# Pair 0 on two load queues with its q in two parts, and inverted sums of pairs 0 to 5 spread by TensorE

## The chip, the cores and the metric

The kernel runs on one core of one Trainium2 chip. The metric is the device time of one execution in microseconds. Three runs of the kernel before took 1489.81, 1485.3 and 1478.97 us; their median is 1485.3 us. One more execution was profiled.

## The reference

Attention with normalized q and k, for 8 batches, 12 heads, 448 tokens and 64 columns per head, and then a bilinear feed-forward block on all 3584 tokens. Everything is fp32.

```python
q_n, k_n = rmsnorm(q, g_q), rmsnorm(k, g_k)          # x / sqrt(mean(x*x) + 1e-6) * g
scores = np.matmul(q_n, k_n.transpose(0, 1, 3, 2)) / np.sqrt(64)
attn = np.exp(scores - scores.max(-1, keepdims=True))
attn = attn / (attn.sum(-1, keepdims=True) + 1e-9)
x = np.matmul(attn, v).transpose(0, 2, 1, 3).reshape(3584, 768)
out = ((x @ w_a) * (x @ w_b)) @ w_out                # 768 -> 1536 -> 768
```

The weights come as fp64 and are rounded to fp32 in the kernel.

## The kernel before

**A pair.** The attention work is cut into 24 units, which the code calls p and this text calls a pair: two pairs of heads of one batch, so four heads. Three units are one batch. For each, `loads` brings q, k and v (two DMAs each, one for each half of the partitions), `normalize` makes the inverse roots of the mean squares, `transposes` turns q and k so that the 64 head columns lie on partitions, `scores` makes seven blocks of scores and their exponentials, `values` multiplies them with v and collects in PSUM.

**Normalization.** ScalarE squares all of q (L434), VectorE reduces it to 14 sums per partition (L436) and scales them (L440), GpSimd raises them to the power -0.5 (L442), VectorE multiplies q with the result (L446). For k the same is done except for the last step: its factor goes into the scale of the exponential (L499). TensorE transposes k and the normalized q, seven blocks of 128 columns each (L472), and ScalarE copies both out of PSUM (L477, L479); the copy of q carries the gains.

**Sums over keys.** Up to pair 4 (`WIDE = 5`) TensorE sums the exponentials over the keys by a product with ones (L551) beside the value products; from pair 5 on, VectorE and GpSimd add the exponentials up first (L529), and one product with ones follows. Each of the 64 partitions of a head then holds the same sums. ScalarE copies them to the tile `rec` (L564). `invert` takes one row for each of two heads, spreads it over 56 partitions of the tile `few` by DMA (L571), VectorE inverts that (L584), a DMA stores it in DRAM (L576), and two DMAs read it back, the same row for 64 partitions each (L580), into `rec`. `divide` multiplies the outputs with it on VectorE (L622). All these DMAs are issued by the queue of SP, in order, among the loads of later pairs.

**PSUM.** The tag `sc` has two buffers of two banks; scores, transposes, and the sums of pairs from 5 on take turns in it. `o` has one (the values), `mm` two of one bank each.

**Weights.** 18 blocks of weights are loaded by ScalarE's queue (L357, L360), rounded (ScalarE L247, VectorE L248 to L256), turned into seven factors (L370) and kept in DRAM (L378, L381). They begin after set points of the attention. The feed-forward block multiplies by quarters with seven products in place of eight (`pq`, L1178; `po`, L879), in the second half of the run twice over (`da` and `dg`, L755; L1076).

**Order.** Every operation is first listed with its engine, a cost, reads and writes; the cost sets nothing any more in this file. `Plan.run` takes a list of places from the packed text `ORDER` (L32) and issues the operations in that order, so each engine's queue is written out by hand, as it were. Waits between engines follow from reads and writes.

**The start.** Five batches of warming matmuls (L1269, four matmuls each of 128 columns, two records to a matmul) run before the first data are there. The first activation (L210) makes ScalarE load its table.

Of the kernel before, what the change touches and what calls it, by code (L numbers as in the profile page):

```python
# [12 lines left out]
FP32 = mybir.dt.float32  # L13
# [7 lines left out]
def _float_of(bits):  # L21
# [11 lines left out]
    "c-rk(33OFulCJ;1>wE9+_r4`BJ4tY13kWE-Vk_=Mzy(Feg+K^|5JDoDg@lB#h!ROcSYk+k7ZAt-gzS(7hD~J+C`N^LVRUq`J$;<<X!jXCGj&5)"  # L33
    ">~_xBo;kMDP5t-X_pkMTRe$|eb)lIZ48gG44VDT<wPl!wVSubDCMZK>O_pV;RFX6)OnL?Ue!mNx-~&&A+nqmLoCL#$X2WBd6NZ@cATDlf_=D%t"
    "xd&3tOb_D{$;`y*kT^Z@O=e006CWR6z%0z0oX2!5-jlniZBcCtG%o}K>tCy^%&H_=J1VNnL92jQVGGP7WJA>&cK!PGq^x2!Dfx~RLvhi!MWenc"
    "O8pvEezjsn4HOlAQTSzHN;DsUva${9%Rbs*8iXx>AKoj2>a}#s7AWo}MX>c4uvHrZP*@2YD*x1x0sFZ2uCM>Y=)}ou;P<=X0+hBC)E6}DBzx+~"
    "&fk5svw3?vsWW%)Y5>?-4?A}3tUdtSYWHnFWYyG?YWV)Uwl3(@zTHGS=x+E5>c52Mop7OX2Q=<)gu1;u;e*=k$3CoWsVx^98p|7C+dgh9w|5Kd"
    "hiXu^(vD^-H8;|R_Qr<Yoshfdv&vRdv7@Q!gAaE?!*-}YSl<J$o~hYhhnrPH6SOuSZ)$7|Y1Uc~G&VHsYiR6hhK^NGzpJ!$N0r!8)pVq)mNx8y"
    "+W)Hk?)#m!wcEE>eNb2R$8)t2HD}LOzx&?%RquV?^X_{+pPYU7d{0l$hsp=<I0EmS2?RE8>7ko9W9{V0(|`O^ccA;5lYx^bjvwy{1kUvQ;q7;h"
    "25QfIdivD)^QTXra=mrx^r=&)1A$ZBuN{63-ad3H(0#D`WMI>q#{yp+ITm>1jV}*X9lmg3@1f5R>^;8!=+V7_qi>!+a&F&Q@#q^>@4oRypr@ni"  # L40
    "O#A6W?d^x#PwYE>@aRA9Yv0@66*%14x#z%Vou7PqY~SAVRb3yof7lT?wCBK~J?9SY-_INj1opSKoZQ=TJkZ?S@$DYy{JL{vTl@aTjV%pb7h0M-"
    "!dg1o&u?t`80uT$+=lf44SOqgy<68&54AgBdtGbwf0j3IZLF?7ux?v9l)qYMwYUGiyzD~Rzrp8g0aim}IoY(U{_LvKRb=(bnrgCADkjB6uN*r`"
    "zFD;bie7&Opl~@Xf7vqO#TNmV(!~@2K3E8OkhcI9<U(!^<PyWk1jv9F=E2+-<^q(aLwXvd&4D?o0JBpd1xzCez`hG)8UdI(1t5MhOnwfYdlsI<"
    ")lUID36tQ7Cm)B2@YqCn6drv99(fpG!gv@DMjXI{500e|*ju~qxf@{2U2xZ(aOZE~PBI#9za4Ia(d0MeR{54ux5$Ky96?45$8ClUg`u&QNnjuh"
    "0JssZ2e__3Kuk15M?q9Sh$5yDhJ;+hNHFokISBFrcs<~8gWCd&fDW3bYm`!@fG(64()|2I`H)9mS^%&hCl_+g6!6(*cDFb`hhzgVD17>o^!!D6"
    "dFcxvH!UZPKx!^zW@KkB%E*Q+an`K&b6_(`%Sz8A88BnroU#|vX3u3|R_f|mv!~DNoUS~d*qS(lBqpSigp`>ub<Wf&*@;u8O><0}o8X)}E&aKv"
    "t`siinRv(3NhQUO8PmC^xCCL+i%%})mOO#<bi>n=o_Hc*(i43A<B!jKoPT8E#BmcJdIsYD>9L7%kHtO4O?YtpqvIw&JZ{|h@sErf|9}`5_wfA_"
    "njW1n_Wp5WvGKszxUu&+#QV5=@4j1jXiVJLxG`hLaQEMJAAdjl;Jx?UkIy~ay?5MwM;kYq=YZwe+gO%&Iry7z8a51sSZ0WD_h5FAK<~JN9nG;E"
    "d+V+2D2_$_F%*UpfgmyVgDS_K2z;Xhw5xcqJidSe%Mg{Jmx{+rsoU+tit(}CR<+(in<eELgXb=lAb$|cvXo^!7R#`VVcKtwVQ`*<aq~Q)0fy}@"
    "p+UHZ2ch^(FD0f$iK<az7sdw2QQd|f#<3v?CMd{8;i1&SPy-DHp_1NWV+NLJy)dI0+K-_=g8bZscqlO}<08vGri3FpB^Ouv2?YE6cFpnvxY0lj"  # L50
    "-EPS;`3_tzXD@Hg)=jo#U#mF)b7w=^#~&xpNls1$v<pauq_^Lm38!a3clTS6cxndx;lzw-N8rsV@UIE+@dx9l?1z6rd|e;D|7<7pU~TtX?4Gvn"
    "?zXnwyW1wULdWZbG&QwBV_W0i#+D}dw5j3yCfL>1@@P}j+4@F!WGC4{-iFgV#@E!;9v@$Qblj06uod7iY~Orfb4|_W>aMPu>d))YLsye+Ra>fR"
    "2yEVZZ&lT%4L$E{J5#;w6m0C?5;y@HV8i;2W7e;$*if-<%)yF^u8Q)GP30E?yLShwssga_)z?TFR0L`(DxhNBn#%I>b?Bzx#PP~w>)))reeJr#"
    "Wrr$Y&B|9{O-ae>RdCyVP+Z(rRJ5XEU0L~ASW~!qb>W&Vg{wA|mIhXDEG4BYS1n&zQUYuDm#ytuQ&PODq<HtL*5a0u;*wh$?%K6t<clMhFD+g6"
    "(z0c@tRPFbyz<J4veAVvkAA6i@k=9?ErOSpE-7AGuy}DHKCLeoE^l~w$%tinI~FgkD_BxcJz`t_;@9%?@<xuz%gYPoF3uhG`oe_;3m2}MKR-V|"
    "uW0`8+`|0a1-aQd3vzRE7Jag~Aa~)mocvsvzd1LjYWV!jto50d*)ZaTjGKnfn?HAM*6N(BtgQB|yzG~=bC(UzdVUF{FUkPq2y@aGq~|=pDYt54"
    "dQLj2%zS=bTH3ty1!<`{>8Zu3rSs>^iOrZjd)|@b^9jsN8<_P%a`No-)Y<51XC<Y~O1^PsDz<0OOi3A#lsxm$%sQH~na+S|a9zTbDG3liB_@96"
    "WE@FKN={CiJbAiJ_)dgrF$vQW6B05q6LVu;jGhb2qcfwP%#50p^=!d28P7zgkf)NLnmH?@Uq6^06*)69DJdaxY66`~BhgKVhK7cRLI?>){~Rp("
    ";32eaH{9yA+~`Y@OheNKX#;P**)%`}MbVXkpa4jiO}U~W3Iq_)1@OVFZTS#kUmHtR`>Sr13{{F0O*0iu@v4e$>AErmTZW=4UVJM`tg2$prYYF;"
    "n95MQrW<;Yq8c7U)m6ocHB`T%5yc~WuxprXhG9~t7_twuJ5`q5gAGGA<RHzk-Mu?j!<M1@JeGU7YH5hTPz_n}sfy-B7}{XdRFIut@msPUtH^FS"  # L60
    "SXNX`))h;`t<51CLX$nc&~8#?)6|t<&HwMXqhD6!FTApB$^(LRJs68AhsPR5s7FSevgTEFTw@|6#dp1o6Lr}dqAAE(lfCvvx@-={wuZ13x1o4%"
    "(k+z3ucGL(td-~%cIa}yP{e~<dHu3?fg*?De!(}$x?9)vVTR$+&0qtoUbk)xGj+FYgczEI9Q_6^@(eZ<12mtE%GcCb*^OdIit1G`0X9`hktBVP"
    "f<1<;j=&zv)KpbL@RG-^N|xloaeaWKOR7IO*sCKCNzn%&Jk3xQQ_@t~7^tXU1fhtw<`vl*gy=K{IpdIo5)YJdF#=H(Su!Qb7%T-zs-1qf+J9y&"
    "9+@WBNj_Qf*&RbrZb{QrpJW3yV>ML1E-R*;wMz(8(gtD>7hKOc8JC06Cy8J>1XdK1rT&6La5!8%&r2c*#2LdnIR`7SGCN_Ygt3is7(qCm;aCwv"
    "OEB=%VG$}|@L>r0d?FIU_ah{n4GRkoBjM=i{bYZTKRO6T1^FUIj`W52Y`5+W@p^qU)a&(lyurldvHW0|UekvbJHTz~mf7E84b2EO4Ng~W^TUv0"
    "0Y-!yCDm!$l~Z;avgDG9Q+E=t(+ie>q?-`UJ9&rd5W;vW@VrmPD5si)<wQ<oLBP<*D>Q`i!ITJK2VaCuNxwS~ILi`-AuN{L?TFYL!|WhUh2KQ+"
    "{Cxu=`5PioFQF0caLO@3te>Sp9-k}J?e;Q^$FvxW8OpddOAlsLl`$2@;gyDjsSIOcxTUNlI-CM3R?v7sp)Sf%o`y4=M6o8Z4$5#*48z(gmZ=xx"
    "GZ)P;3`Z4=?>NKBMwzVW0-_L+RU|<YqF7#36b#A&%epw$!Lw>ON+2@C(cej(h@4R{^t*_RQgZ#!b+Dq$5}r~_2`K-4G>c)FK^!Q$NEjiS(HU0#"
# [78 lines left out]
def kernel(  # L147
# [35 lines left out]
    nc = tc.nc  # L183
# [24 lines left out]
    def setup():  # L208

        nc.scalar.activation(grow, nc.const_aps.tensor(0.0, [1, 4, D], FP32), AF.Exp)  # L210
        make_identity(nc, ident)
        nc.gpsimd.memset(expo, -0.5)
        nc.gpsimd.memset(ones, 1.0)
# [61 lines left out]
    def fast_body(ld, wk, ps_s, ps_o, ps_mm, dram):  # L275
# [8 lines left out]
        WARM = 5  # L284
# [8 lines left out]
        WIDE = 5  # L293
# [104 lines left out]

        xs, rs, qns, qkTs, pts, scs, ETs, sums, sus, os_, quads, hTs = ({} for _ in range(12))
        low_high = [slice(0, D), slice(D, P)]  # L400

        def loads(p, nm):
            b, h0 = p // HC, 4 * (p % HC)
            src = {"q": q, "k": k, "v": v}[nm]
            t = tile_of(f"{nm}{p}", nm, 2 if nm == "v" else 1)

            def emit():
                x = ld.tile([P, NT, 2, D] if nm == "k" else [P, 2, NT * D], FP32, tag=nm, name=nm + "_sb", bufs=2 if nm == "v" else 1)
                for w in range(2):
                    pair = src[b, h0 + 2 * w:h0 + 2 * w + 2]  # L410
                    nc.sync.dma_start(x[low_high[w]], pair.rearrange("h (p j) d -> p j h d" if nm == "k" else
                                                                     "h (p j) d -> p h (j d)", j=NT))
                xs[nm, p] = x
            op("SP", 1.28 if nm != "k" else 1.4, p - (1.8 if nm == "v" else 2.0), emit, [f"firsts{PREP}"] if p >= HELD else [], [t], new=[t],
               kb={"q": 690, "k": 770, "v": 530}[nm], dmas=2)

        def normalize(p):
# [8 lines left out]
            def squares(s, nm):  # L426
# [8 lines left out]
                op("ACT", 0.95, key, square, [f"{nm}{p}"], [sq], new=[sq])  # L435
                op("DVE", 1.1, key, lambda: nc.vector.tensor_reduce(rs[p][:, s], xs["sq", nm, p], AX, ALU.add), [sq], [f"{ms}/{nm}"])  # L436

# [6 lines left out]
            def apply():  # L444
# [5 lines left out]
                    ALU.mult)  # L450
            squares(0, "q")
# [10 lines left out]
        def transposes(p):  # L462

            qkT, key = tile_of(f"qkT{p}", "qkT", 2), p - EARLY
            for n, nm in ((1, "k"), (0, "q")):
# [18 lines left out]

        def scores(p, j):
# [982 lines left out]
```

## Time and profile before

| what | before |
|---|---|
| median of three runs | 1485.3 us |
| profiled execution | 1483.15 us |
| its span, first to last instruction | 1481.3 us |
| TensorE busy | 1460.9 us (99%) |
| VectorE busy | 983.6 us (66%) |
| ScalarE busy | 437.3 us (30%) |
| GpSimd busy | 320.6 us (22%) |
| DMA | 250.75 MB, 169 GB/s |
| mean granted TensorE clock | 0.995 |

The profile is of one execution. Its times count from the first instruction. An engine is busy while an instruction is in it; a matmul that waits inside the array counts as busy, too. A group is given as line, engine, operation, what it writes and reads, shape and count; an idle time in brackets is that of the engine before the instruction, with what ended it. "x16" counts records; an fp32 matmul leaves two.

### The profile page before, as it was taken

The page shows a single profiled execution, that of the slowest core. Times are in us where ns is not written, and L with a number is a line of the kernel's source. Part 1 is how long each engine was busy: PE and PEld are TensorE (multiplying, and loading weights), DVE is VectorE, ACT ScalarE, POOL GpSimd, SP SyncE. Part 2 cuts the span into 40 slices and gives each one's busy share as a digit, 9 for nine tenths or more (in the row PEclk, how much of TensorE's full clock was granted, in tenths as well). Part 3 has the DMA queues.
Part 4 walks back from the last instruction along what each step waited for, and adds up shares of the span by engine and source line. Part 5 has one row for each costly group of instructions (what it writes and reads, how often), then busy time and mean ns, then how long its engine had stood idle before and what let it go on. Part 6 is the DMA issues. An engine that isn't in the chain of part 4 may idle for free.

```text
span 1481.3 us, 20985 instructions
## 1 busy us (share of the span) xinstructions
PE 1460.9 (99%) x7854; PEld 957.9 (65%) x7854; DVE 983.6 (66%) x1568; ACT 437.3 (30%) x790; POOL 320.6 (22%) x172
## 2 busy tenths in 40 slices
PE   8999999999999999999999999999999999999998
PEld 5433345555445555555544445799998899999898
DVE  5897688888685233334666865457686676777785
ACT  5777762111563000000167771011111011111100
POOL 3326543111342001101255541011120001121000
PEclk9999999999999999999999999999999999999999
DMA  9898446644352453755656444655555765555455
GB/s 261 245 275 241 102 106 202 216 154 179 125 146 68 142 160 124 217 167 160 182 167 179 121 129 137 183 155 160 163 177 167 253 177 159 166 154 171 152 182 146
DMA packets 189075, 250.75 MB, mean 169 GB/s; under 512 B 61988, under 2 KB 160804, under 8 KB 182308
## 3 DMA queue, kind: packets, MB, share of 16 engines
q1 hardware_dynamic: 160900, 195.82, 46.3%
q10 hardware_dynamic: 28064, 53.48, 10.6%
q8 instruction: 65, 1.06, 0.3%
q14 instruction: 46, 0.38, 0.1%
HBM read 191.10 MB, written 57.97 MB: 168 GB/s over the span
## 4 chain that ended last, share of the span: by engine, by line
PE 88%; ACT 1%; DVE 1%; issue 0%; DMA 0%; SPq 0%; DVEq 0%; ACTq 0%
PE pq L1178 25%; PE dg L755 17%; PE po L879 16%; PE da L755 6%; PE sc L493 6%; PE o L515 6%; PE a L1076 2%; PE g L1076 2%; PE pt L472 2%; PE e L1076 1%; PE d L1076 1%; PE b L1076 1%; PE su L551 1%; DMA q_sb<-in_q_dram 0%; ACT ET L499 0%
## 5 line engine op out<-in xcount | busy, mean ns | idle before, releaser
L1178 PE MATMUL pq<-x,st 128*128 128x448 f32 x1008 | 382.2, 540 | 0.9 <-DVE U L1208 0.9
L1178 PEld LDWEIGHTS pq<-x,st 128*128 128x128 f32 x1008 | 190.3, 190 | 188.8 <-issue 180.4
L499 ACT ACTIVATE ET<-sc,ms 128x448 f32<-128x448 f32 x336 | 190.6, 635 | 88.3 <-PE sc L493 70.9
L442 POOL TENSOR_TENSOR ms<-ms,expo 128x14 f32<-128x14 f32 x48 | 143.4, 2996 | 134.7 <-DVE ms L440 134.1
L755 PE MATMUL dg<-dT,st 128*128 128x224 f32 x672 | 168.7, 353 | 0.0
L493 PE MATMUL sc<-qkT 64*64 64x448 f32 x1344 | 159.8, 552 | 7.0 <-ACT ET L499 4.2
L755 PE MATMUL dg<-x,st 128*128 128x224 f32 x672 | 164.9, 353 | 0.0
L879 PE MATMUL po<-st,hT 128*128 128x384 f32 x492 | 163.7, 487 | 0.0
L515 PE MATMUL o<-ET,v_sb 64*64 64x448 f32 x1344 | 151.9, 544 | 1.1 <-ACT ET L499 1.1
L783 POOL TENSOR_TENSOR hT<-dF 128x448 f32<-128x448 f32 x42 | 48.3, 1164 | 421.5 <-DVE dF L778 421.5
L879 PEld LDWEIGHTS po<-st,hT 128*128 128x128 f32 x492 | 92.4, 190 | 64.9 <-issue 3.9
L755 PEld LDWEIGHTS dg<-dT,st 128*128 128x128 f32 x672 | 126.8, 190 | 1.3 <-DVE dt L795 0.4
L755 PEld LDWEIGHTS dg<-x,st 128*128 128x128 f32 x672 | 126.5, 190 | 1.7 <-DVE dF L802 1.3
L755 PE MATMUL da<-x,st 128*128 128x224 f32 x504 | 118.5, 353 | 0.1
L529 POOL TENSOR_TENSOR sum<-sum,ET 128x896 f32<-128x896 f32 x38 | 84.2, 2215 | 131.5 <-DVE sum L529 77.7
L493 PEld LDWEIGHTS sc<-qkT 64*64 64x64 f32 x1344 | 46.7, 134 | 94.3 <-issue 40.4
L515 PEld LDWEIGHTS o<-ET,v_sb 64*64 64x64 f32 x1344 | 52.4, 134 | 75.3 <-issue 64.7
L755 PEld LDWEIGHTS da<-x,st 128*128 128x128 f32 x504 | 94.5, 190 | 1.5 <-ACT dt L768 0.7
L778 DVE TENSOR_TENSOR dF<-dF 128x896 f32<-128x896 f32 x84 | 92.5, 1105 | 2.7 <-DVE dF L807 0.5
L768 ACT COPY dt<-da 128x224 f32<-128x224 f32 x84 | 29.0, 346 | 210.1 <-PE da L755 130.8
L879 PE MATMUL po<-st,fin 128*128 128x384 f32 x252 | 87.0, 492 | 0.0
L1226 POOL TENSOR_TENSOR hT<-hT,t 128x448 f32<-128x448 f32 x12 | 14.1, 1172 | 300.1 <-DVE t L1224 300.1
(136 smaller groups left out, 1706.6 us busy)
## 6 DMA issues: line engine op xcount, KB each, us to landing
st<-kept_o SPq DMA_DIRECT2D x28, 1152.0 KB
st<-kept_s SPq DMA_DIRECT2D x84, 320.0 KB
kept<-st ACTq DMA_DIRECT2D x12, 1344.0 KB
st<-kept SPq DMA_DIRECT2D x12, 1344.0 KB
st<-kept SPq DMA_DIRECT2D x84, 192.0 KB
ti<-kept_t SPq DMA_DIRECT2D x48, 288.0 KB
kept_s<-ds SPq DMA_DIRECT2D x30, 448.0 KB
q_sb<-in_q_dram SPq DMA_DIRECT2D x48, 224.0 KB
```

Of the source, the lines that this page charges most:

```text
L442: lambda: nc.gpsimd.tensor_tensor(msf(), msf(), expo[:, 0:2 * NT * (b - a)], ALU.pow), [], names)
L472: nc.tensor.transpose(t[:, j * P:(j + 1) * P], x[:, j].rearrange("p h d -> p (h d)"), ident)
L493: nc.tensor.matmul(t[low_high[w], e, 0:S], lhsT=qkTs[p][low_high[e], 1, j * P + w * D:j * P + (w + 1) * D], rhs=qkTs[p][low_high[e], 0, w ...
L499: nc.scalar.activation(E[:, e], scs[p, j][:, e, 0:S], AF.Exp, scale=rs[p][:, 1, 2 * j + e:2 * j + e + 1])
L515: nc.tensor.matmul(os_[p][low_high[e], w, 0:S], lhsT=xs["v", p][low_high[w], e, j * D:(j + 1) * D], rhs=ETs[p, j][low_high[w], e], start=( ...
L529: two[e].tensor_tensor(sums[p], sums[p] if j > 1 else ETs[p, 0], ETs[p, j], ALU.add)
L755: nc.tensor.matmul(to(), lhsT=W(w), rhs=t(), start=not more and k == 0, stop=k == len(terms) - 1, skip_group_check=True)
L778: take("DVE", 1.09, lambda: V.tensor_tensor(F[to], F[to], F[other], ALU.add), allF(other), allF(to), lock=True)
L783: lambda: two[e].tensor_tensor(C(i, n), F[g][:, 0:S], F[g][:, S:2 * S], ALU.mult), allF(g),
L879: nc.tensor.matmul(held["po"][:, 0:HALF], lhsT=a[0]()[:, c], rhs=sts[beta, 12 + place_of[f]][:, c], start=(c == 0), stop=(c == MH - 1))
L1076: nc.tensor.matmul(held[bank], lhsT=x()[:, c], rhs=y(c), start=(start and c == 0), stop=(stop and c == MI - 1), skip_group_check=True)
L1178: nc.tensor.matmul(banks[bank][:, 0:S], lhsT=sts[at][:, f, c * P:(c + 1) * P], rhs=quads[x][:, c], start=(start and c == 0), stop=(stop an ...
```

## The change

1. q and k of pair 0 are loaded by SP and ScalarE, a half of the partitions each, in place of both by SP. The first activation, with the table load, writes the tile `gain` (one column) in place of `grow`, and is an operation of the list.
2. q of pair 0 goes through squares, sums, power, product, transposes and copy in two parts, of four and three blocks (`front`, `turn_first`). Three warming batches in place of five stand at the start, and four stand among the transposes: one after k's, one after the first part of q, two after the second. The scores of pair 0 come after them.
3. For pairs 0 to 5 the inverted sums are no longer stored in DRAM and read back for 64 partitions. Two DMAs bring the two inverted rows back to one partition each (`rows`), and four matmuls with ones spread each over 64 partitions in PSUM, in a buffer of `sc` (`spread`). `divide` reads them there.
4. `ORDER` is another text.

```diff
-    "c-rk(33OFulCJ;1>wE9+_r4`BJ4tY13kWE-Vk_=Mzy(Feg+K^|5JDoDg@lB#h!ROcSYk+k7ZAt-gzS(7hD~J+C`N^LVRUq`J$;<<X!jXCGj&5)"
...
+    "-I8N<`#|1qx2F9!6o&rN"
...
-        nc.scalar.activation(grow, nc.const_aps.tensor(0.0, [1, 4, D], FP32), AF.Exp)
...
-        WARM = 5
+        WARM, SPLIT = 3, ((0, 4), (4, NT))
+        TAIL = {("k", None): 1, ("q", 0): 1, ("q", 1): 2}
...
-        WIDE = 5
+        WIDE, SPREAD = 5, 6
...
+        op("ACT", 1.7, -9, lambda: nc.scalar.activation(gain, nc.const_aps.tensor(0.0, [P, 1], FP32), AF.Exp), [], ["gain"])
...
+                def half(w):
+                    pair = src[b, h0 + 2 * w:h0 + 2 * w + 2]
+                    queue[("SP", "ACT")[w]].dma_start(
+                        xs[nm, p][low_high[w]], pair.rearrange("h (p j) d -> p j h d" if nm == "k" else "h (p j) d -> p h (j d)", j=NT))
...
+            def front(n):
+                j0, j1 = SPLIT[n]
+                a, c = 2 * j0, 2 * j1
...
+                op("ACT", 0.1 + 0.85 * share, -9, square, loaded(0, "q"), [f"{sq}/{n}"], new=[sq] if n == 0 else [])
+                op("DVE", 0.14 + 0.96 * share, -9, lambda: nc.vector.tensor_reduce(msf(), xs["sq", "q", 0][:, a:c], AX, ALU.add),
+                   [f"{sq}/{n}"], [mine])
+                op("DVE", 0.2, -9, lambda: nc.vector.tensor_scalar(msf(), msf(), 1.0 / D, 1e-6, ALU.mult, ALU.add), [], [mine])
+                op("POOL", 0.2 + 2.5 * share, -9,
+                   lambda: nc.gpsimd.tensor_tensor(msf(), msf(), expo[:, a:c], ALU.pow), [], [mine])
...
+                op("DVE", 0.15 + share, -9, times, [mine] + loaded(0, "q"), [f"qn0/{n}"], new=["qn0"] if n == 0 else [], lock=True)
...
+        def turn_first():
...
+                op("PE", 0.95 * size, -9, turn, (loaded(0, "k") if n is None else [f"qn0/{n}"]) + ["heat"], [pt, "heat"], new=[pt], mode="full")
+                op("ACT", 0.1 + 0.9 * size, -9, take, [pt] + ["gain"] * (n is not None), [f"qkT0/{1 if n is None else f'0{n}'}"],
+                   new=["qkT0"] if n is None else [])
+                for x in range(TAIL[nm, n]):
+                    op("PE", 0.5, -9, warm, ["warm", "heat"], ["warm", "heat"], mode="full")
...
-            op("PE", 0.76, p, product, [f"qkT{p}/0", f"qkT{p}/1"], [sc, f"at{p}.{j}"] + ([f"half{p}"] if j == NT // 2 else []), new=[sc],
+            op("PE", 0.76, p, product, ["qkT0/00", "qkT0/01", "qkT0/1", "heat"] if p == 0 else [f"qkT{p}/0", f"qkT{p}/1"], [sc, f"at{p}.{j}"] + ([f"half{p}"] if j == NT // 2 else []), new=[sc],
...
+            def rows():
+                for e in range(2):
+                    nc.sync.dma_start(sus[p][e * D:e * D + 1].rearrange("o w s -> o (w s)").rearrange("o (p i) -> o p i", p=FEW),
+                                      fews[0][e * FEW:(e + 1) * FEW])
+
+            def spread():
+                t = ps_s.tile([P, 2, 512], FP32, tag="sc", name="inv")
+                for w in range(2):
+                    for e in range(2):
+                        nc.tensor.matmul(t[low_high[e], w, 0:S], lhsT=ones[e * D:e * D + 1, :], rhs=sus[p][e * D:e * D + 1, w],
+                                         start=True, stop=True)
+                sus[p] = t[:, :, 0:S]
...
+            if p < SPREAD:
+                op("SP", 1.3, p, rows, [few], [t], kb=8, dmas=2)
+                inv = tile_of(f"inv{p}", "sc", 2)
+                op("PE", 0.76, p, spread, [t], [inv], new=[inv], mode="quad")
+                return
...
-                op("DVE", 0.65, p, emit, [f"rec{p}"], [f"{x}/{c}"], lock=True)
+                op("DVE", 0.62 if p < SPREAD else 0.65, p, emit, [f"inv{p}" if p < SPREAD else f"rec{p}"], [f"{x}/{c}"], lock=p >= SPREAD)
```

## The prediction

> **What bounds the kernel now.** I read the page first, then the busy time by stretches, then the timeline of the first 20 us and of 60 to 86 us. On the page TensorE is busy all the time:
>
> ```profile
> PE 1460.9 (99%) x7854; PEld 957.9 (65%) x7854; DVE 983.6 (66%) x1568; ACT 437.3 (30%) x790; POOL 320.6 (22%) x172
> PE 88%; ACT 1%; DVE 1%; issue 0%; DMA 0%; SPq 0%; DVEq 0%; ACTq 0%
> ```
>
> Busy is not yet full rate, so I ask in which stretch TensorE gets through fewer records than it could. The columns are: stretch in us, busy us (and records) of PE, weight load, DVE, ACT and POOL, the granted clock, DMA share and GB/s.
>
> ```profile
> 0.00:14.48 14.48, 9.53 (x57) 8.88 (x57) 4.22 (x9) 5.47 (x7) 6.00 (x10) 0.97 0.90 226
> 14.48:20.46 5.98, 5.98 (x33) 2.43 (x37) 1.37 (x2) 3.69 (x5) 0.00 (x0) 0.51 1.04 309
> 20.46:79.50 59.04, 55.36 (x534) 23.97 (x526) 51.87 (x62) 43.59 (x66) 20.26 (x7) 1.00 0.90 249
> 79.50:85.50 6.00, 5.43 (x38) 2.42 (x40) 5.91 (x6) 4.59 (x10) 1.37 (x1) 0.72 1.09 289
> 85.50:166.60 81.10, 76.79 (x735) 31.41 (x727) 62.14 (x81) 64.65 (x105) 39.65 (x15) 1.00 0.83 225
> 240.00:370.00 130.00, 130.00 (x347) 65.61 (x346) 113.00 (x131) 20.25 (x21) 16.79 (x12) 1.00 0.53 188
> ```
>
> From 240 to 370 us a record of 448 columns on the whole array takes 130/347 = 0.375 us without a gap. The attention products are on quarters of the array (64*64), four abreast, so each record is worth a quarter, 0.094 us (the chain shows 16 such records in 1.50 us). At that price 534 records from 20.46 to 79.5 are some 50.7 us of 59.0, transposes included; 735 from 85.5 to 166.6 are 73.2 of 81.1 (12 of them on the whole array); 33 from 14.48 to 20.46 are 3.1 of 6.0; 38 from 79.5 to 85.5 are 3.6 of 6.0. With the 14.5 us before the first score the first 167 us hold some 36 us in which TensorE gives less than full rate, or nothing. After that it is nearly full until the end, so **time won or lost before 167 us goes through to the end nearly whole**, and matmuls added there cost their length unless they fall into a gap.
>
> What the gaps wait for:
>
> ```profile
> 5.49 0.95 ACT L434 ACTIVATE sq<-q_sb 128x896 f32<-128x896 f32 x1 [3.04 <-DMA q_sb<-in_q_dram]
> 7.92 5.15 POOL L442 TENSOR_TENSOR ms<-ms,expo 128x14 f32<-128x14 f32 x2 [6.47 <-DVE ms L440]
> 10.55 1.09 DVE L446 TENSOR_TENSOR qn<-q_sb,ms 128x896 f32<-128x896 f32 x1 [0.23 <-POOL ms L442]
> 12.60 0.91 ACT L477 COPY qkT<-pt 128x896 f32<-128x896 f32 x1
> 14.48 3.27 PE L493 MATMUL sc<-qkT 64*64 64x448 f32 x16 [1.79 <-ACT qkT L479]
> 16.38 1.16 ACT L499 ACTIVATE ET<-sc,ms 128x448 f32<-128x448 f32 x2 [1.95 <-PE sc L493]
> ...
> 60.83 1.66 SPq L571 DMA_DIRECT2D few<-rec  x2
> 68.33 0.25 DVE L584 RECIPROCAL few<-few 112x16 f32<-112x16 f32 x1 [3.19 <-DMA few<-rec]
> 76.84 1.66 ACT L247 ACTIVATE st<-lraw 128x1536 f32<-128x1536 f32 x1 [3.39 <-DVE ms L436]
> 79.59 0.98 PE L493 MATMUL sc<-qkT 64*64 64x448 f32 x8 [1.34 <-ACT ET L499]
> ```
>
> Above: one serial chain for q of pair 0 leads to the first score at 14.48. Below: sums sent out by 62.5 land at 68.3 (5.8 us); VectorE stands 3.19 us; its weight rounding is late; ScalarE, which must issue the next weight load (at 75.80, once VectorE has read the old words), stands 3.39 us with the exponentials behind that; TensorE stands, and the next clock window is half (0.72 over 79.5 to 85.5).
>
> [...] TensorE works less than half of 8.6 to 14.48 us, and the clock is 0.51 from 14.48 to 20.46. [...] The two q issues take 1.46 us here[...].
>
> **The change, part by part.**
>
> *Front.* q's halves are issued together instead of 0.73 us apart: q lands at about 4.9 instead of 5.45 (-0.5; nothing if ScalarE's issue falls behind its table load of 1.28 us). Nothing else that is due stands on that queue: the first weight load goes at 5.51 already. SP is freed of 1.4 us, so k, gains and v follow sooner. The parts are 4/7 and 3/7 of rows that I have: square 0.95, reduction 1.09, scaling 0.17, power 2.6, product 1.09, transposes 0.98, copy 1.01. First part: 4.9, square to 5.5, reduction to 6.3, scaling to 6.5, power (1.6) to 8.2, product to 9.0, transposes to 9.7. Second part: its power (1.3) follows the first's to 9.5, product to 10.2, transposes to 10.8, copy to 11.4. But two warming batches stand after the second transposes on TensorE, ahead of the scores: 2 x 8 records of 128 columns, 0.107 us each at full clock, 1.7 us. So the first score is at about 12.6, not 11.4. The third power, k's, ends at 9.5 + 2.6 = 12.1, ahead of that. First exponential: 12.6 + 0.75 + 0.3 = 13.6 against 16.38, -2.7. If the clock stays full, ScalarE's 1.43 us behind scores at 21.5 goes too. I take **-4.1**. Bounds: power's price for 8 and 6 elements isn't in the trace; if it is all fixed (2.6 each) the front wins 0.8; if the clock is half, the warming batches take 3.4 us and it wins nothing; if everything fits, -6. The smaller table-loading activation lies under ScalarE's 3.04 us wait: 0.
>
> *Spreading by TensorE, pairs 0 to 5.* Each gets four K=1 products of 448 columns. The added code takes the SBUF row and the PSUM half both from e, so only two quarters are used, each twice, one after the other: 2 x 0.75 = 1.5 us, not the 0.76 that the code's cost says. Six: **9.0 us** on an engine that sets the end. Cover: the waits for exponentials before 125 us, of 0.4 to 1.8 us (40.7, 59.5, 79.6, 118.2 and smaller). Half: **+4.5**. Ends: +9 uncovered, 0 if all falls in gaps.
>
> *PSUM.* The result sits in one of the two score buffers until both divides are done: 1.5, then 2 x 0.62, then up to 1.77 for the weight step that VectorE is in, some 4.5 us. In that time score, exponential, score run one by one, 0.75 + 0.2 + 1.16 = 2.1 us a step; a step of TensorE with its value and sum products is 2.25, so pairs 0 to 4 lose little; pair 5 has no sum products then and loses 0.6 a step. **+0.8**, up to +4. The divide out of PSUM: 0.62, as L1206 (0.620) reads PSUM: 0.
>
> *DMA.* Six stores and twelve broadcasts go (64 rows of 3.5 KB, 229 KB each, 2.75 MB; at 249 GB/s 11 us of transfer in a stretch at 0.9 share); twelve row loads of 3.5 KB come, on SP ahead of the next pairs' loads. SP then waits once a pair (for the inversion) instead of also for the store's landing (35.3 us in 19 waits over the run), so loads behind it go sooner, but mostly wait for their buffers. First products on pairs 0 to 5 come late (pq from 128 us on), so an earlier inverse is no gain itself. Fewer waits like the 3.19 us: **-1.0**, 0 to -4.
>
> *Sequence.* It is written as packed text; I read no places from it. Known stall it could cure: the 68 us chain, 1.34 + 0.49 us and 1.7 of half clock, 3.5. I take half, **-1.8**; -8 to +8 elsewhere, with no reason for a sign.
>
> Sum: -4.1 + 4.5 + 0.8 - 1.0 - 1.8 = -1.6. The profiled execution took 1483.15 us (span 1481.3), so 1481.6, rounded **1482**. The median of the three runs, 1485.3, is 2.2 above it, and they spread over 10.8; about 1% is what a measurement of this kernel can tell from no change.
>
> **Rivals.**
> 1. *The gaps take it all*: all spreads covered (-4.5) and the 68 us chain gone whole (-1.7), with 3 more of DMA relief: 1482 - 9 = 1473. For it: 16 us of gaps in 20 to 167. Against: those gaps come when ScalarE is late, not where a row has just landed.
> 2. *TensorE waits for the rows.* The spread waits in order for a load; all scores and values stand behind it. Today no TensorE instruction waits on that trip: only VectorE does, for `few`, at 3 of 7 places in the front. Small transfers land 5.8 us after issue there, while the plan's constant for landing is 1.65. Where less than some 5.8 us of TensorE work lies between inversion and spread, the rest is lost: 4.1 us x 3 of 6 = 12, and with half clock once after it 1.5: 1482 + 13 = 1495, slower than before. It decides from about 0.6 us a pair on.
> 3. *The front doesn't come*: half clock, power at its fixed price: 1482 + 4.1 = 1486.
>
> **Chances.** Likeliest 0.45 (1476 to 1488 alone), rival 1 0.23, rival 2 0.19, rival 3 0.13. Faster by over 1% (under 1470.4) takes two fifths of rival 1 and a little of the likeliest: 0.11. Slower by over 1% (over 1500.2): a third of rival 2 and some unknown sequence: 0.08. Within: 0.81. Range 1470 to 1495: it leaves out the better part of rival 1's lower half and of rival 2's upper.
>
> **What would show it.** First score near 12.6 and granted clock full up to 20 us (front). Spread matmuls: 48 records, 1.5 us a pair, `sc` after them late (cost). TensorE idle "<-DMA rec" (rival 2). VectorE's idle before L584 small, ScalarE's 3.39 gone (sequence). Busy PE records from 240 us on at 0.375 again; if they aren't, or if pairs come in another order over the first 400 us, the prediction is wrong for a reason not named here.

## The result and the profile after

The changed kernel takes 1488.06 us (median of 20 executions, 1483.63 to 1492.87); beside it, on the same chip, the kernel before takes 1485.26. The ratio is **1.0022, 95% interval 1.001 to 1.0034**: some 3 us slower, where 1.6 us faster was forecast. The profiled execution of after happens to be its longest: 1492.87 us, span 1491.1, 9.7 us over the profiled one of before, while the medians differ by 2.8. So a profile tells here *where* time goes, and only medians how much. One execution of all those below, of e3, took 2594.87 us at a mean granted clock of 0.555, and its ratio leaves that one out.

The first and fourth part of the page, after:

```profile
PE 1469.9 (99%) x7918; PEld 964.2 (65%) x7918; DVE 985.9 (66%) x1571; ACT 438.7 (29%) x792; POOL 333.2 (22%) x173
PE 89%; DMA 5%; DVE 3%; issue 1%; ACT 1%; SPq 1%; POOL 0%; ACTq 0%; DVEq 0%; POOLq 0%
```

TensorE is still what is busy; DMA is now 5% of the chain (k of pair 0, 7.83 us, and the rows of pair 3, 7.82 us, are pieces of it), where it was 0%. The stretches of after (us; busy us and records of PE, weight load, DVE, ACT, POOL; granted clock; DMA share; GB/s):

```profile
0.00:9.00 9.00, 4.89 (x24) 4.70 (x24) 1.65 (x6) 2.33 (x3) 1.21 (x9) 0.99 0.80 192
9.00:20.00 11.00, 9.25 (x64) 8.11 (x64) 3.01 (x5) 4.88 (x8) 5.40 (x3) 0.69 1.10 269
20.00:110.00 90.00, 88.27 (x872) 38.75 (x864) 78.74 (x93) 68.80 (x106) 31.87 (x9) 1.00 0.85 247
110.00:131.70 21.70, 18.09 (x133) 6.55 (x133) 15.46 (x18) 13.66 (x23) 10.07 (x3) 0.84 0.67 175
240.00:370.00 130.00, 130.00 (x358) 65.27 (x357) 110.99 (x129) 20.30 (x21) 21.78 (x15) 1.00 0.55 190
```

and the third and fourth stretch in the kernel before:

```profile
20.00:110.00 90.00, 85.74 (x819) 37.10 (x815) 80.81 (x94) 67.51 (x105) 27.10 (x9) 0.98 0.95 262
110.00:131.70 21.70, 20.88 (x194) 9.26 (x186) 16.05 (x22) 17.56 (x28) 14.18 (x5) 1.00 0.96 282
```

From 240 us on both run at full rate, so the difference lies before. From 20 to 110 us after gets through 872 records where before did 819, 24 of them spreads. From 110 to 131.7 it gets through 133, eight of them spreads, where before did 194: **one place is where most is lost in this execution**.

To compare stretches I price each record at full rate, as the prediction did (0.375 us for 448 columns on the whole array, a quarter of that on 64*64, and so on), leave warming and spreads out, and call the rest of the elapsed time *shortfall*. By 20 us it is 15.5 us before and 17.0 after; by 40 us 18.2 in both; by 110 us 28.6 and 27.5; by 130 us 30.2 and 37.0; by 240 us 40.1 and 48.4 (9.0 of it spreads). In all profiles below the time less the shortfall by 240 us lies between 1443.0 and 1444.9 us: nearly all that differs between these kernels happens before 240 us.

**The front.** Timeline of after:

```profile
2.19 0.70 ACTq L358 DMA_DIRECT2D hraw<-in_moe_w_out_dram  x1
2.79 0.64 SPq L432 DMA_DIRECT2D k_sb<-in_k_dram  x1
5.30 1.28 ACT L473 ACT_TABLE_LOAD   x1 [5.30 <-DMA q_sb<-in_q_dram]
6.60 1.04 ACT L473 ACTIVATE sq<-q_sb 128x512 f32<-128x512 f32 x2
8.64 2.95 POOL L489 TENSOR_TENSOR ms<-ms,expo 128x8 f32<-128x8 f32 x2 [7.18 <-DVE ms L487]
10.75 1.72 PE L561 MATMUL pt<-ident,k_sb 128*128 128x128 f32 x7 [4.50 <-DMA k_sb<-in_k_dram]
18.78 1.74 PE L585 MATMUL sc<-qkT 64*64 64x448 f32 x16
```

The first weight load (`hraw`) goes at 2.19 us, not 5.51, ahead of k's second half; k is there at 10.72, not 8.05. The table load (5.30 us) comes after q has landed. TensorE stands 4.50 us for k, the clock is half from 8.9 to 15.7 us, and the first score starts at 18.78 us; 12.6 was forecast, 14.48 it was.

**Pair 3.** Timeline of after, from its reciprocal on:

```profile
116.22 0.25 DVE L689 RECIPROCAL few<-few 112x16 f32<-112x16 f32 x1
116.49 1.68 SPq L672 DMA_DIRECT2D rec<-few  x2
124.45 4.26 PE L679 MATMUL inv<-rec,ones 1*64 1x448 f32 x8 [1.77 <-DMA rec<-few]
128.64 1.77 PE L585 MATMUL sc<-qkT 64*64 64x448 f32 x8
128.75 0.97 ACT L656 COPY rec<-su 128x448 f32<-128x448 f32 x2 [4.75 <-PE inv L679]
128.75 1.15 DVE L732 TENSOR_TENSOR x<-x,inv 128x448 f32<-128x448 f32 x2 [4.90 <-PE inv L679]
```

Two rows of 3.5 KB, issued by 118.2 us, land at 124.4 and 125.5; TensorE, with all that follows in its order behind the spread, stands; then the clock is half until 131.7 us and the spread takes 4.2 us instead of 1.65; ScalarE and VectorE wait for it. This is the prediction's second rival, at one pair of six. At the other pairs the spread is what the first step of that sum said: 1.65 us from start to next product (50.37 to 52.02), where that sum has 1.5.

### The profile page after: what moved, and what is told of

It is laid out like the page before. It is cut to its first block, busy times and chain, and to the rows that moved or that the text cites. A ratio compares the mean times of both kernels' runs of the same rounds, so it can differ in the third digit from the quotient of the medians.

```text
span 1491.1 us, 21095 instructions
## 1 busy us (share of the span) xinstructions
PE 1469.9 (99%) x7918; PEld 964.2 (65%) x7918; DVE 985.9 (66%) x1571; ACT 438.7 (29%) x792; POOL 333.2 (22%) x173
## 4 chain that ended last, share of the span: by engine, by line
PE 89%; DMA 5%; DVE 3%; issue 1%; ACT 1%; SPq 1%; POOL 0%; ACTq 0%; DVEq 0%; POOLq 0%
PE pq L1288 24%; PE dg L865 17%; PE po L989 16%; PE sc L585 7%; PE o L607 7%; PE da L865 6%; PE g L1186 2%; PE a L1186 2%; PE pt L537 2%; PE su L643 2%; DMA k_sb<-in_k_dram 2%; PE b L1186 1%; PE d L1186 1%; PE e L1186 1%; PE inv L679 1%
## 5 line engine op out<-in xcount | busy, mean ns | idle before, releaser
L498 POOL TENSOR_TENSOR ms<-ms,expo 128x14 f32<-128x14 f32 x47 | 149.2, 3175 | 149.2 <-DVE ms L496 148.2
L585 PE MATMUL sc<-qkT 64*64 64x448 f32 x1344 | 153.0, 545 | 2.0 <-ACT ET L591 1.7
L607 PE MATMUL o<-ET,v_sb 64*64 64x448 f32 x1344 | 148.9, 542 | 0.0
L621 DVE TENSOR_TENSOR sum<-sum,ET 128x896 f32<-128x896 f32 x57 | 62.8, 1101 | 30.0 <-POOL sum L621 18.8
```

The costliest lines, as they stand in the source:

```text
L498: lambda: nc.gpsimd.tensor_tensor(msf(), msf(), expo[:, 0:2 * NT * (b - a)], ALU.pow), [], names)
L585: nc.tensor.matmul(t[low_high[w], e, 0:S], lhsT=qkTs[p][low_high[e], 1, j * P + w * D:j * P + (w + 1) * D], rhs=qkTs[p][low_high[e], 0, w ...
L607: nc.tensor.matmul(os_[p][low_high[e], w, 0:S], lhsT=xs["v", p][low_high[w], e, j * D:(j + 1) * D], rhs=ETs[p, j][low_high[w], e], start=( ...
L621: two[e].tensor_tensor(sums[p], sums[p] if j > 1 else ETs[p, 0], ETs[p, j], ALU.add)
```

## The experiments

Each ran beside the kernel before, on the same chip (e1 to e4 on one, the others on another), and the ratio is to that. *Shortfall* is by 240 us of the profiled execution, with the spreads in it in brackets; *half clock* the time at half of the full clock in it, the last microseconds left out.

| kernel | median us | ratio, 95% | profiled us | first score | shortfall | half clock |
|---|---|---|---|---|---|---|
| before | 1485.3 | 1 | 1483.2 | 14.5 | 40.1 | 10.2 |
| after | 1488.1 | 1.0022 (1.001 to 1.0034) | 1492.9 | 18.8 | 48.4 (9.0) | 13.7 |
| e1 front mended | 1486.3 | 1.0013 (1.0004 to 1.0021) | 1485.5 | 15.6 | 41.6 (9.0) | 10.2 |
| e2 spread doubled | 1501.5 | 1.0112 (1.0095 to 1.0128) | 1502.3 | | 59.2 (18.0) | 27.3 |
| e3 spread alone | 1504.0 | 1.0125 (1.0108 to 1.0143) | 1503.9 | | 60.4 (9.0) | 30.7 |
| e4 front alone | 1486.5 | 1.0014 (1.0006 to 1.0022) | 1487.3 | 19.3 | 43.9 | 10.2 |
| e5 pair 3 early | 1483.2 | 1.0 (0.9988 to 1.0012) | 1481.8 | 15.7 | 37.1 (9.0) | 3.4 |
| e6 four quarters | 1486.4 | 1.002 (1.001 to 1.0029) | 1486.2 | | 43.1 (4.5) | 10.2 |
| e7 mended front alone | 1485.2 | 1.0009 (0.9998 to 1.002) | 1486.5 | 17.1 | 43.1 | 10.2 |
| e8 no spread | 1505.1 | 1.0149 (1.0128 to 1.0171) | 1504.8 | | 60.4 | 30.7 |
| e9 q before rows | 1488.9 | 1.0032 (1.0019 to 1.0046) | 1483.1 | | 38.2 (4.5) | 0 |
| e10 longer warming | 1487.8 | 1.002 (1.0009 to 1.003) | 1486.3 | | 43.1 (4.5) | 6.8 |
| e11 two quarters | 1482.8 | 0.999 (0.9982 to 0.9999) | 1482.0 | 14.4 | 37.5 (9.0) | 0 |
| e12 later square | 1481.7 | 0.9982 (0.9973 to 0.9991) | 1481.2 | 14.7 | 37.1 (9.0) | 0 |

e1 to e4, e5 to e8 and e9 to e11 ran side by side, e12 by itself. Operations are moved in the written order by this edit, with pairs "operation, operation before which it now stands":

```diff
-        for k in range(n):
-            x = rest.pop(places[k] + 256 * places[n + k])
+        seq = [rest.pop(places[k] + 256 * places[n + k]) for k in range(n)]
+        for x, y in MOVES:
+            seq.remove(x)
+            seq.insert(seq.index(y), x)
+        for k, x in enumerate(seq):
```

### The front mended

The changed kernel with k's second half ahead of the gains on SP, the table-loading activation ahead of the squares, and the first three weight loads behind the squares and k's copy:

```diff
+MOVES = ((25, 9), (1, 34), (11, 39), (12, 45), (64, 29))
```

> Theory F: the first score moved from 14.48 to 18.78 us because the first weight load is issued at 2.19, between the halves of k, and the table load stands behind q; with k's halves first, the weight loads back behind the squares and the table load before q is there, k lands near 7.5 us in place of 10.7, the first score comes near 14 us, and the total falls by 3 to 5 us, to some 1484. Rival P (pair 1 sets the pace and a late pair 0 is caught up by 40 us, where both traces have 21.66 us of products done): the first score comes near 14 us as well, but the total stays at 1488 within 1.

Measured: 1486.26 us, ratio 1.0013 against after's 1.0022. k lands at 8.2 us, first score at 15.55. At 110 us the shortfall is 23.4 us, 5.2 better than before; at 130 us it is 31.4, 1.2 worse. The wait for rows at pair 3 is there too (TensorE idle 1.53 us until 118.68, half clock 118.4 to 125.3). Neither expectation came about (3 to 5 us faster, or 1488 within 1). By the ratios the order in the front costs about 1.3 us (1.0022 to 1.0013), but their intervals overlap, so this size isn't settled; in the profile the front's lead doesn't outlive pair 3.

### The spread twice

```diff
-                for w in range(2):
+                for w in (0, 1, 0, 1):
```

> The four spreading products of pairs 0 to 5 are made twice, which adds 1.5 us of TensorE work to each of six pairs. If spreads cost their length: plus 9, to 1497. If half of it falls into gaps, as I took it: plus 4.5, to 1492.5. If the gaps take it all: 1488.

Measured: 1.0112 against 1.0022, 13.4 us for 9.0 us of added matmuls, more than any of the three expectations. On balance nothing of the added length was covered: the cover of one half that the prediction allowed isn't there for more of it. The half clock doubles, from 13.7 to 27.3 us, and not only where TensorE stands. At three places (53.6, 152.6 and 173.1 us) it begins after 3.4 us in which TensorE was busy throughout; the first of them, with the 3.4 us after it (same columns as above):

```profile
50.19:53.61 3.42, 3.42 (x23) 1.72 (x23) 0.52 (x1) 0.95 (x1) 1.37 (x1) 1.00 0.64 153
53.61:57.02 3.41, 3.41 (x24) 1.14 (x20) 3.38 (x5) 0.00 (x0) 0.00 (x0) 0.50 1.08 368
```

What fills most of the first of these lines is the doubled spread (from 49.29 to 52.99 us), products of one row.

### The spread alone, in the old sequence

The kernel before, with `rows` and `spread` for pairs 0 to 5, each spread just ahead of its divides:

```diff
-        WIDE = 5
+        WIDE, SPREAD = 5, 6
...
+MOVES = ((235, 236), (335, 336), (435, 436), (505, 506), (575, 576), (634, 635))
```

> The kernel before with the spread by TensorE alone (pairs 0 to 5, each spread right ahead of its divides, all else in the old sequence). If spreads cost their length and the lighter DMA load gives nothing: 1485.3 plus 9, 1494. With half covered and 1 us of relief: 1489. If TensorE waits for the rows as it does at pair 3 in the changed kernel: more waits ended by rec<-few in the trace, 1497 or more.

Measured: 1504.0 us, 1.0125. Its stretches around the first spread, at 55.0 us (same columns as above):

```profile
50.00:58.20 8.20, 7.48 (x68) 2.42 (x64) 5.79 (x7) 4.58 (x8) 4.11 (x2) 1.00 0.91 269
58.20:68.40 10.20, 8.66 (x45) 3.69 (x49) 7.61 (x11) 6.12 (x10) 2.82 (x1) 0.50 0.51 158
```

No wait for rows occurs, so the third expectation has the size (1497 or more) but not the reason, and the other two are exceeded. The spread ends at 56.7 us; with one of the two score buffers taken, the next score but one waits for its exponential (1.34 us, until 58.98), and the half clock sets in at 58.2, in the middle of that wait, for 10.2 us. The 3.4 us ahead of it hold the spread and 0.55 us of the wait: both can have a part, and this run doesn't separate them. Over the whole run the half clock grows from 10.2 to 30.7 us, worth 10.2 us; with the 9.0 us of spreads that is 19.2, and the profiled times differ by 20.8. So here the spread costs its full length and once more that in clock.

### The front alone

The change's front up to pair 0's second score, then the old sequence (another text in `ORDER`), sums through DRAM for all pairs.

```diff
-        WIDE, SPREAD = 5, 6
+        WIDE, SPREAD = 5, 0
```

> The new front of pair 0 as in the change up to its second scores, then the old sequence, no spread by TensorE. Theory F: first score near 18.8 us, total 1485.3 plus 2 to 4, 1487.5 to 1489.5. Rival P: caught up by pair 1, 1485.3 within 1.

Measured: 1486.5 us, 1.0014: **2.1 us slower** than before, where the prediction had the front at -4.1.

### Pair 3's rows earlier

The mended front, and pair 3's reciprocal and row loads earlier in the sequence:

```diff
+MOVES = ((25, 9), (1, 34), (11, 39), (12, 45), (64, 29), (517, 163), (518, 557))
```

> The kernel with the mended front and, besides, pair 3's inversion and row loads earlier in the sequence, so that its spread finds its rows there. Theory (the row wait at pair 3 and the half clock after it, 1.7 and some 3.4 us, are what the mended front's lead of 5 us at 110 us was lost to): 1481 to 1483, no idle stretch of TensorE with rec<-few as its end before 130 us, half clock once less. Rival (the wait goes elsewhere, or the stretch of 110 to 130 us is short of exponentials and not of rows): 1486 as with the mended front alone.

Measured: 1483.2 us, ratio 1.0. The profile's view of the spread matmuls (duration in ns, min/median/max; first and last start in us) in after, and in this kernel:

```profile
L679 PE MATMUL inv<-rec,ones x48: 533/535/1003, 50.4 to 165.3; 1*64 1x448 f32 x48
```

```profile
L685 PE MATMUL inv<-rec,ones x48: 534/534/585, 48.2 to 154.3; 1*64 1x448 f32 x48
```

No spread runs at half clock any more, none waits for its rows, and half clock is left in one stretch of 3.4 us at 9 us. From 1.0022 (after) to 1.0 is 3.3 us, all that after loses, and just clear of the noise (0.0022 with an uncertainty of 0.0017): the two mendings together take the loss away. How it divides is less sure. From e1's 1.0013 to 1.0 is 1.9 us by the ratios, 3.1 by the medians, and the intervals overlap; so 1.3 for the front and some 2 for pair 3 are estimates.

### Four quarters

As e5, with each row brought in two halves onto both partitions, so that the four products of a pair use four quarters:

```diff
-                for e in range(2):
-                    nc.sync.dma_start(sus[p][e * D:e * D + 1].rearrange("o w s -> o (w s)").rearrange("o (p i) -> o p i", p=FEW),
-                                      fews[0][e * FEW:(e + 1) * FEW])
+                for e in range(2):
+                    for w in range(2):
+                        r, few = (e ^ w) * D, e * FEW + w * FEW // 2
+                        nc.sync.dma_start(sus[p][r:r + 1, w].rearrange("o (p i) -> o p i", p=FEW // 2), fews[0][few:few + FEW // 2])
...
-                        nc.tensor.matmul(t[low_high[e], w, 0:S], lhsT=ones[e * D:e * D + 1, :], rhs=sus[p][e * D:e * D + 1, w],
-                                         start=True, stop=True)
+                        r = (e ^ w) * D
+                        nc.tensor.matmul(t[low_high[e], w, 0:S], lhsT=ones[r:r + 1, :], rhs=sus[p][r:r + 1, w], start=True, stop=True)
```

> As the one with pair 3 earlier, and each pair's row brought by four half-row loads onto both partitions, so that its four spreading products use four different quarters of the array and run four abreast. Theory (the spread costs its length, 1.5 us a pair because only two quarters are used): 0.75 us a pair, 4.5 us in all, come back: 1477 to 1479; the pair's spread lasts 0.8 us in the trace. Rival (two more issues a pair on the sync queue, 0.7 us each, make the rows or the later loads late): 1482 or more, with TensorE waiting for rows at one of the pairs.

Measured: 1486.4 us, 1.002: slower than e5, though the spread does shrink where its rows are there, to 0.91 us from start to next product (75.20 us) against 1.65. With each of the four K=1 products on another pair of SBUF half and PSUM half, they run abreast here. The timeline shows where it goes:

```profile
84.99 3.32 SPq L680 DMA_DIRECT2D rec<-few  x4
89.08 1.36 SPq L429 DMA_DIRECT2D q_sb<-in_q_dram  x2
97.21 0.95 ACT L467 ACTIVATE sq<-q_sb 128x896 f32<-128x896 f32 x1 [4.57 <-DMA q_sb<-in_q_dram]
99.26 1.77 PE L591 MATMUL sc<-qkT 64*64 64x448 f32 x8 [2.88 <-ACT ET L597]
```

Four issues take 3.3 us of SP; q of a later pair goes at 89.1 and lands at 97.2; ScalarE, whose next instruction is that q's square, stands 4.57 us with exponentials behind it; TensorE stands 2.88 us, and half clock follows. The rows are late as well, as the rival said: at pair 3 the last half rows land inside the spread, which takes 3.23 us (121.47 to 124.70), and half clock follows there too (125.9 to 129.3).

### The mended front alone

As e4, with the front's order of e1. The moves are those of e1, here written into `ORDER` itself:

```diff
+MOVES = ((25, 9), (1, 34), (11, 39), (12, 45), (64, 29))
```

> The kernel before with the change's front in its mended order (second half of k ahead of the gains, table load ahead of the squares, first weight loads behind k), sums brought back as before through DRAM, old sequence after the front. Theory (the changed front's flaws cost some 3 us against its mended form, and what it wins is then consumed by nothing): 1483 to 1484 against the 1486.5 of the front alone; first score at 15.5. Rival (the front's time is caught up in the next 60 us whatever it is): 1486, as the front alone.

Measured: 1.0009, its interval reaching to 1. First score 17.1 us, not the 15.5 expected: 6.8 us of half clock follow TensorE's 2.6 us without work ahead of k's transposes here (3.4 us in e1, after 1.82). By 40 us its shortfall is that of before, 18.2. **The new front, in either order, wins nothing ahead of the old sequence.**

### The new sequence without the spread

After, its sums of pairs 0 to 5 brought back through DRAM as before, each broadcast 13 operations behind its store:

```diff
-        WIDE, SPREAD = 5, 6
+        WIDE, SPREAD = 5, 0
...
+MOVES = ((249, 74), (349, 443), (449, 564), (519, 560), (589, 949), (648, 972))
```

> The changed kernel in its new sequence and with its front as it is, but the inverted sums of pairs 0 to 5 brought back by broadcasts through DRAM as before, no spread. Theory (spreads cost their 9 us of TensorE, and at pair 3 a wait and a half clock of 5 us more; the new sequence itself is worth that much): 1474 to 1479. Rival (the new sequence is only good with the spreads, VectorE waits for the broadcasts as in the kernel before): 1485 or more, VectorE idle before the divides.

Measured: 1505.1 us, 1.0149. Its timeline:

```profile
59.47 0.95 ACT L467 ACTIVATE sq<-k_sb 128x896 f32<-128x896 f32 x1 [5.77 <-DMA k_sb<-in_k_dram]
61.95 1.77 PE L591 MATMUL sc<-qkT 64*64 64x448 f32 x8 [4.97 <-ACT ET L597]
88.81 0.62 DVE L738 TENSOR_TENSOR x<-x,rec 128x448 f32<-128x448 f32 x1 [7.61 <-DMA rec<-inv]
91.10 2.19 PE L649 MATMUL su<-ET,ones 64*64 64x448 f32 x8 [8.24 <-ACT rec L662]
```

The rival: the new order has no room for the trip through DRAM. SP's queue is late with k, VectorE waits 7.61 us for a broadcast, TensorE stands. Where I put the broadcasts is part of this, as where I put the spreads is part of e3, so neither is a price of the sequence or of the spread by itself. With these places, either without the other loses 19 to 22 us by the ratios, where both together lose 3.

### q ahead of the rows

As e6, pair 5's q load ahead of pair 2's row loads and pair 3's row loads ahead of pair 6's k:

```diff
+MOVES = ((25, 9), (1, 34), (11, 39), (12, 45), (64, 29), (517, 163), (518, 622), (563, 448))
```

> The kernel with four quarters, with two places in the sequence changed: pair 5's q load ahead of pair 2's row loads on the sync queue, and pair 3's row loads ahead of pair 6's k load. Theory (what the four quarters gained, 4.5 us, went into q of pair 5 landing late behind the four row issues, ScalarE standing 4.57 us with exponentials behind it, and two half clocks of 3.4 us): 1486.4 - 3.3 - 3.4 = 1479 to 1480, no stall of TensorE above 1 us between 90 and 130 us. Rival (the gain goes into the next wait, whichever transfer is then last): 1483 or more.

Measured: 1488.9 us, 1.0032. In the profiled execution the stall at 99 us is gone, but the rival holds further on, at pair 6's k, which now goes after four row issues:

```profile
119.56 0.95 ACT L467 ACTIVATE sq<-k_sb 128x896 f32<-128x896 f32 x1 [3.22 <-DMA k_sb<-in_k_dram]
121.61 0.98 PE L591 MATMUL sc<-qkT 64*64 64x448 f32 x8 [2.87 <-ACT ET L597]
```

The same stall of 2.9 us, this time without a half clock, and 1483.1 us; but that is the fastest of eight executions (to 1492.7), and the only one with a profile. The median didn't fall (1488.9 against 1486.4). That the gain went into the next wait fits the profile; for the slower executions it isn't shown.

### Longer warming, and two quarters again

The first has e9's order and five products (10 records) instead of four in each of the three first warming batches; the second has the same and the change's own `rows` and `spread`:

```diff
-                    op("PE", (2.5, 1.7, 1.7)[x] if x < 3 else 0.9, 1e6, warm, ["warm"], ["warm"], mode="full")
+                    op("PE", (2.5, 1.7, 1.7)[x] if x < 3 else 0.9, 1e6, lambda: warm(5), ["warm"], ["warm"], mode="full")
```

> As the one with q ahead of the rows, and each of the three warming batches at the start one fourth longer (10 products in place of 8), so that TensorE works until some 7.6 us and not 6.2. Theory (the half clock of 9 to 12.5 us is the answer to the 1.8 to 2.2 us in which TensorE waits for k): no half clock in the first 20 us, 1.5 us less than without. Rival (the clock there is set by more than this gap, for instance by the work being thin up to 15 us): the same time within 1 us, half clock as before.

> As the one with longer warming, but with the change's own spread (two row loads, two quarters). Theory (spreading on two quarters costs 0.75 us a pair more when nothing else is late): 4 to 4.5 us above the four quarters, 1482 to 1483. Rival (two fewer issues a pair on the sync queue are worth as much as 0.75 us of TensorE): within 1.5 us of the four quarters.

Measured: 1487.8 us and 1482.8. In both the clock is full in the first 20 us; but it was so in the profile of e9 as well, so e10 doesn't tell what the longer warming is worth (1.1 us by the medians, within the intervals). The pair tells more: **the same kernel with two row loads and two quarters is 5.0 us faster than with four and four**, where 4 us slower was expected. In e10's profile half rows land late inside pair 2's spread (two of the four issues go 1.9 us after the first two, at 89.94; TensorE is idle 2.24 us at 95.35), and half clock follows. At pair 3 of e6 they did, too. That two more small loads a pair cost more than the 0.75 us that they save is shown; that it is by this way in most executions isn't.

### The square later

As e11, the squares of pair 2's q behind two exponentials and the copies of pair 0's sums, and the steps that follow later too:

```diff
+MOVES = (..., (312, 255), (313, 71), (314, 71), (315, 247), (320, 318))
```

> As the one with two quarters and longer warming, and the squares of pair 2's q (with the reduction, the power and the product that follow) behind two exponentials and the copies of pair 0's sums, so that ScalarE doesn't stand on q's load at 33 to 36 us (2.85 us there). Theory (executions differ because a late load lands in front of queued exponentials, and this is the first such place): the stall of 1.55 us at 37 us gone, and 1480.5 to 1482; a ratio to the kernel before of 0.998. Rival (the time is caught up later, or the wait moves to the product or the transposes of that q): 1482 to 1484, as the one it is made from.

Measured: 1481.7 us, **0.9982 (0.9973 to 0.9991)**: faster than before, by 2.7 us. Of e11 (0.9982 to 0.9999) it can't be told apart. The timeline at that place in e11, then in e12:

```profile
36.05 0.95 ACT L467 ACTIVATE sq<-q_sb 128x896 f32<-128x896 f32 x1 [2.85 <-DMA q_sb<-in_q_dram]
37.47 1.40 PE L649 MATMUL su<-ET,ones 64*64 64x448 f32 x8 [1.11 <-ACT rec L662]
```

```profile
37.98 0.95 ACT L467 ACTIVATE sq<-q_sb 128x896 f32<-128x896 f32 x1 [1.77 <-DMA q_sb<-in_q_dram]
40.03 0.98 PE L591 MATMUL sc<-qkT 64*64 64x448 f32 x8 [1.37 <-ACT ET L597]
45.65 0.96 PE L543 MATMUL pt<-ident,qn 128*128 128x128 f32 x7 [1.47 <-DVE ms L502]
```

The stall at 37 us is gone, but the wait has moved, as the rival said: TensorE stands 1.37 us for an exponential behind the same square, and 1.47 us ahead of the transposes of that q. By 48 us the shortfall is 18.0 us in both profiles. So the moved square isn't shown to win anything; what e12 gains on before, it has in common with e11 (the mended front, pair 3's rows in time, longer warming); what each adds beyond e5's 1.0 isn't separated.

In e10 the same load, issued by 27.9 us (27.7 in e11), landed 2 us later (38.2 us); a stall of 2.97 us and a half clock followed. That this is why executions of one kernel lie 7 to 11 us apart is argued from these two profiles, not shown.

## Why the prediction was wrong

The forecast was -1.6 us, the result +3.3 by the ratio; it lies in the range given. By steps:

- **Front, -4.1: this step failed.** Alone it is +2.1 (e4; 0.9 to 3.3 by the interval), 6.2 us off, more than the whole error of 4.9. Three terms in it were wrong. First, "Nothing else that is due stands on that queue: the first weight load goes at 5.51 already": the weight load goes at 2.19. It was held back by naming `k0` as read; the change writes `k0/0` and `k0/1` instead, so that name has no writer but the buffer's opening, and the load is free to go ahead of k. That it is free could be read in the diff; that it goes ahead stands only in the packed `ORDER`, from which the prediction read no places. Second, "The smaller table-loading activation lies under ScalarE's 3.04 us wait: 0": it is an operation of the list now and stands behind the squares (11.58 us), so the table load of 1.28 us comes after q has landed. Third, full clock to 20 us: TensorE has 4.50 us without work before k, and the clock is half from 8.9 to 15.7. The power for 8 and 6 elements was sized right: 2.95 us for both. Even with the first two mended, the first score starts at 14.4 to 17.1 us (e1, e5 to e7, e9 to e12). In e12, at full clock throughout, q's squares start at 5.56 us (5.49 before): the two queues bring nothing. Its power starts at 7.60 and not 6.5, since VectorE reduces both parts before it scales either, and its product at 10.32 and not 8.2, since k's sum of squares (9.32, 1.08 us) is ahead of it on VectorE, whose order the sum had left out. With 1.95 us of warming in front of the score that makes 14.65. This is the third rival's outcome, a front that doesn't come, by a way that it names only in part: half clock yes, a fixed price of the power no.
- **Spreads, 9.0 us of work, +4.5 net.** The work was right (48 records, 1.5 us a pair). The cover of one half has no support: in the old sequence the cost is 19 us (e3), doubling it costs 13.4 for 9.0 (e2). What the spread does to the clock was no term of the sum: in e2 half clock follows three stretches in which nothing but the doubled spread kept TensorE from full work. That after is nevertheless only 3.3 us slower fits that it spares the trip through DRAM in a sequence written for that (e8); this is argued, since e8's own places are part of its loss.
- **PSUM buffer, +0.8, up to +4.** In the old sequence the loss isn't the 0.6 us a step that was priced. Beyond the spreads' length it is mostly half clock: 20.5 us more of it, worth 10.2 (e3). Each of the five stretches of 3.4 us ahead of it holds a spread and 0.5 to 1.3 us in which TensorE stands. What of that is due to the taken buffer is open. In the new sequence it doesn't show.
- **DMA -1.0 and sequence -1.8**, together with the two above +2.5. Measured as after less the front alone: 1.0022 to 1.0014, +1.2 with an uncertainty of about 2, if the parts add up. So the rest of the sum came out near its value, which is in part luck, since the parts are others: some +2 of it is pair 3's rows, the second rival at one pair: there TensorE had work for 6.2 us after the reciprocal (116.47 to 122.68), more than the 5.8 that this rival asked for, but the trip of the two rows took 8 to 9.
- ScalarE's wait of 3.39 us at 75 us and the half clock after it are gone in after, as the last step hoped, but ScalarE stands 3.71 us until 53.75 for a q load in their place. Up to 110 us after is 1.1 us ahead.
- The test "if pairs come in another order over the first 400 us" did not apply, and records from 240 us on take 0.375 us, as said (0.363 as a mean in after, where 16 of the 358 are on quarters).

## What to carry to other kernels

When an operation's output is split, look for every other operation that named the whole: an ordering hint without a writer releases what it held, here a 768 KB load onto the queue in front of the data that the start waits for. When a wait by an engine that is not the bound (VectorE for a broadcast) becomes a wait by the bound itself (TensorE for a row), price the trip by what small transfers take under load (here 8 to 9 us from the first issue to use, at pair 3 of after), and see that this much work lies between in *every* repetition; one of six was enough. A matmul saved can cost more than it is worth if it is paid for with more issues on a queue that feeds the bound: 0.75 us a pair saved against two more loads a pair lost 5.0 us here (e10 against e11). And products that use one row of the array can cost clock even where they fill a gap in time: doubling them took the half clock of the profiled executions from 13.7 to 27.3 us here (e2).

## What was not expected of the hardware

- Half clock comes where TensorE never stands, too. In these profiles it comes in stretches of 3.4, 6.8 and 10.2 us (81.83 to 85.25 us and 13.57 to 20.39 in before, 58.2 to 68.4 in e3), at a granted clock of 0.50. In e3 20.5 us more of it and 9.0 us of spreads go with 20.8 us more of time, so an estimate from these figures makes it worth about half its length here. In e2 TensorE is busy for all of the 3.42 us ahead of the half clock at 53.6 us, for 2.80 of them with products of one row (1*64).
- TensorE's busy share does not tell where half clock comes. It is 1.00 in that stretch of e2; in after it is 0.48 from 121.52 to 124.93 us (1.64 of 3.41, at full clock), and 6.83 us at 0.50 follow; and it is 0.42 in this stretch of e9, whose profile has no half clock before its last microseconds:

```profile
119.64:123.06 3.42, 1.45 (x16) 0.67 (x20) 1.60 (x2) 3.17 (x6) 1.42 (x1) 1.00 0.48 131
```

- So equal stalls can differ. After the 2.88 us of e6 at 99 us eight records of scores take 1.77 us, at half clock; after the 2.87 us of e9 at 122 us they take 0.98. What decides between the two isn't shown, and no run was made to test it.
- The landing of one and the same q load took 8.3 us from the end of its issue in one profile and 10.3 in another (e11, from 27.7 us; e10, from 27.9).
- Two POOL powers, for 8 and 6 elements on 128 partitions, take 1.65 and 1.33 us, together about as much as the one for 14 behind them (2.82; 2.58 to 4.09 in the kernel before): here its time goes with the elements.
